# Another order for a hand-ordered attention stage, with the next tile's flags read inside it

## The chip, the cores and the metric

The kernel runs on one core of a Trainium2 chip, as one launch. The core has five engines, each with an instruction queue that is worked off in order: TensorE (PE) multiplies matrices, VectorE (DVE), ScalarE (ACT) and GpSimd (POOL) work on tiles in on-chip memory, and SyncE (SP) issues transfers (DMAs) between the chip's main memory and the tiles; ScalarE and GpSimd can issue transfers too. An engine waits for another by semaphores. The metric is the device time of a launch in microseconds (us), the median of several runs.

## The reference

Three layers follow each other: an attention between x and a small state, in both directions; a mixture of experts, where each row goes to the one expert that its largest logit names; and a dense layer with a gated activation.

```python
# x (4,8,512,64), state (4,8,32,64)
a  = softmax(x @ state.T / 8);  xread = a @ state
a2 = softmax(state @ x.T / 8);  sread = a2 @ x
x = concat([xread, sread], axis=2) -> 2176 rows of 512
# 8 experts, w1 (8,512,1024), w2 (8,1024,512), each takes its first rows up to a capacity
e = argmax(x @ w_gate);  g = softmax(x @ w_gate)[e]
x = g * (relu(x @ w1[e]) @ w2[e])          # rows beyond the capacity are 0
# dense layer, w_in (512,2048), w_out (2048,512)
h = x @ w_in
out = (h * clip(h + 3, 0, 6) / 6) @ w_out
```

## The kernel before

**The stages.** The first, here called the ordered stage, computes the attention for the four batches, writes its rows to the scratch tensor `x_rows`, sorts the rows by expert, and computes the first tile of 256 rows of the mixture. It ends at about 90 us. Then a Python loop over five more tiles of the mixture (`for s in range(N0, NF)`) runs `m1` (L904: rows times w1, in two pieces `q` per group) and `m2` (L922: times w2). Rows that don't fill a tile go in two "pairs", half a tile for each of two experts, with loops of their own (`p_m1` L1254, `p_m2` L1280). The dense layer (L1314, L1352) and the scatter of its rows (L1489) follow from about 240 us on.

**What sets the order.** The ordered stage is written as generators (`tr`, `scores`, `soft_max`, `read_sum`, `lists`, `tables`, `e_m1` and others), each yielding after one or a few instructions. The table `ORDER` names, word by word, which generator takes its next step (`name*3`: three steps); with that an instruction's place in each engine's queue is fixed. Batch b is in the name, as in `tr10` for batch 1. A set of names, `ALT`, chooses the engine of single operations: `mul` and `sub` (L327, L314) and the one-hot tests `oh` (L539) run on VectorE if they are named and else on GpSimd; `rd`, an eviction of attention rows, on VectorE (L404) if named and else on ScalarE (L406); the weight residual `wp` (L827) on GpSimd if named and else on VectorE. Behind the stage the code's own order holds.

**The start.** `inputs` loads the state in two parts with `state_in` (L137): the first quarter `st2[:, 0:2]`, 64 KB, from ScalarE's queue, the rest from SyncE's, between the loads of x (L101, `xb`), which go in pieces of one head. VectorE copies both parts to `aT` (L163, L167); PE transposes the copy (`pst`, L246), VectorE writes it scaled to `sT` (L254), and with `sT` and the transposed x (`psx` L277, copied to `xT` by L279) PE computes the scores (`pss`, L285).

**Weights.** Each tile loads four pieces of w1 (`r0`) and four of w2 (`r1`), 512 KB each, on SyncE (L815, `raw`). ScalarE casts a piece to the reduced format (L825, `w1h` or `w2h`) and a second engine takes the residual (L827, `w1l` or `w2l`), so that a product is three matmuls. Two integers from the table `tab` decide: a flag whether the tile's expert is a new one, and its number. Loads whose flag is zero are skipped, and the split stands in a branch that all engines evaluate. `flags(i)` reads the two integers into SyncE's registers. A pair takes its two experts from the table `tabh` (`p_experts`, L1210) and loads eight pieces of w1, later eight of w2, straight into spare buffers (`p_loads`).

**The end of the stage.** VectorE works the tables out (`tables` up to L709, `halves` up to L782) between the last steps of the first tile, whose result is evicted in two halves (L932) to a tile `y` (here named `xb`) and written by SyncE to the scratch tensor `y_pad` (L938). `next_rows`, `next_turn` and `next_gates` prepare tile 1. Behind the stage, `flags` of tiles 1 and 2, `loads` of `r0`, the first two loads of the dense layer's weights (`vload`, L1112 and L1114, tile `st`), the branch, `r1` of tile 1, `listed`, and `p_begin` with the pair's reads and loads stand in this order.

Of the kernel before, what the change touches and what calls it, by code (L numbers as in the profile page):

```python
# [29 lines left out]
    setup0*4 inputs setup0 tr00 prep_state0 setup2*2 prep_state0*2 setup2*2 setup0 tr00 setup0 tr01 setup2*2 consts tr01 scores00 tr03 tr02 setup2*2  # L30
    inputs zeros setup1 setup3*2 setup1*2 soft_max00 soft_exp00 setup3 setup2 setup1 setup3*2 setup2*2 prep_state2 setup2 turn00 read_max00 setup2
    tr03 e2_turn00 setup2 inputs read_max00 tr02 scores01 e2_turn00 setup2 read_exp00 tr10 turn01 tr11 read_max01 prep_state2 tr10 tr11 setup3
    soft_max01 prep_state2 read_max01 soft_exp01 setup2*2 setup3 setup2 s_read00 read_exp01 prep_state2*2 setup3 setup2 setup3 setup2 inputs s_read00
    read_sum00 s_read00 setup3*2 setup2 read_sum00 read_sum01 prep_state2 scores10 tr12 read_sum00 read_sum01 consts setup2 read_sum01 e2_turn01 tr12
    prep_gate tr20 soft_max10 e2_turn01 tr13 turn10 read_sum00 read_max10 setup3 s_read01 read_sum01 tr20 tr13 prep_gate tr21 soft_exp10 scores11
    inputs s_scale0 tr21 read_max10 s_scale0 read_turn00 read_exp10 read06 setup2 read_turn01 scores20 setup2 turn11 soft_max11 setup3 read_sum10 tr22
    soft_exp11 tr23 read_max11 s_turn0 read_sum10 read_init0 soft_max20 read_max11 read00 turn20 tr22 tr23 read06 read_sum10 read04 scores21 read00
    read07 setup2 s_read10 read_sum10 s_turn0 read05 read_max20 read04 read_exp11 turn21 read01 read07 e2_turn10 read_turn10 read_max21 read_max20
    read03 read05 read02 soft_max21 read_sum11 read_exp20 read01 s_logits0 read_max21 read03 s_read10 setup2 setup3 read02 read10 s_logits0 e2_turn11
    rows_out0 e2_turn10 setup3 read_sum11 read_init1 count0*2 setup3 soft_exp20 count0 e2_turn11 read_sum11 count0 setup3 count0 tr30 s_read10  # L40
    read_sum11 first_expert tr30 before0 first_expert read_exp21 s_logits0 read16 tr31 count0 setup3 first_expert read_sum20 first_expert tr33
    first_expert before0 first_expert s_read11 read_sum20 first_expert read16 tr31 s_scale1 before0 first_expert tr33 first_expert read_turn11 setup3
    total0 soft_exp21 tr32*2 sums0 rows_out0 first_expert read10 place0 scores30 place0 read_sum21 place0 e2_turn20 e2_turn21 s_read20 read12 s_ids0
    place0 read14 read_sum20 s_scale1 place0 soft_max30 turn30 read15 s_scale0 place0 read_sum20 read_init2 read_max30 place0 e2_turn20 read_sum21
    e2_turn21 read_max30 s_turn1 scores31 lists0 read14 read12 s_read20 read15 place0 s_turn1 place0 read_sum21 turn31 soft_max31 lists0 read_max31
    read17 read11 read_sum21 read17 read13 soft_exp30 s_read21 read_exp30 read_turn21 read_turn20 lists0 e2_turn30 early s_logits1 raws lists0 raws
# [554 lines left out]
def full(ctx, tc, x, state, w_gate, w1, w2, capacity, w_in, w_out, out, dbg=None):  # L601
# [343 lines left out]
    def tiles(wk, sm, pS, pT, okp):  # L945
# [703 lines left out]
```

## Time and profile before

| | us |
|---|---|
| median of 3 runs | 559.38 (559.15 to 559.63) |
| the profiled execution | 558.27 |
| its span, first to last instruction | 556.6 |
| PE busy in the span | 525.8 (94%) |
| VectorE busy | 299.5 (54%) |
| ScalarE busy | 217.9 (39%) |
| GpSimd busy | 143.6 (26%) |

The span is what the profiler saw between the first and the last instruction; the execution's own time has 1.7 us round it. The mean granted clock of TensorE is 0.987 of full speed. Shares are averages over three different stages, so what a change in one of them does must be read from that stage: which wait ends last there. "Idle before" in a row is the time that an engine stood still ahead of an instruction, with the name of what let it go.

### The profile page before, as it was taken

The numbers are of one execution on the slowest core, as the hardware profiler recorded it, in microseconds if no ns is written. First come the engines' busy times: TensorE is split into PE (matmuls) and PEld (weight loads), VectorE is DVE, ScalarE is ACT, GpSimd is POOL, SyncE is SP. The second block draws the span as 40 slices with busy tenths as digits, with TensorE's granted clock in tenths as the row PEclk, the third lists the DMA queues.
The fourth block names the chain that finished last, engine by engine and source line by source line (L and its number), as shares of the span: only waits on it lengthen the run. The fifth ranks groups of instructions, "written<-read, shape, count | busy, mean of one in ns | idle before, by whom it ended". The sixth has DMA issues, their size and how long they took to land.

```text
span 556.6 us, 10122 instructions
## 1 busy us (share of the span) xinstructions
PE 525.8 (94%) x3772; PEld 462.8 (83%) x3772; DVE 299.5 (54%) x729; ACT 217.9 (39%) x461; POOL 143.6 (26%) x198
## 2 busy tenths in 40 slices
PE   3899998988999999999999999999999999999990
PEld 1566998958969898999999889999999998888880
DVE  3799894339626763766879852243343343322340
ACT  2788751235214331434443443333333343332340
POOL 1546764113401010136777722001001001000002
PEclk9999999998999999999999999999999999999996
DMA  6727723998989785247653411011001010000001
GB/s 135 179 97 259 253 87 118 315 351 268 378 305 376 253 317 163 77 152 249 228 187 114 134 38 58 1 38 39 1 20 57 1 31 19 21 0 1 0 21 50
DMA packets 52169, 74.99 MB, mean 135 GB/s; under 512 B 23089, under 2 KB 31537, under 8 KB 51602
## 3 DMA queue, kind: packets, MB, share of 16 engines
q1 hardware_dynamic: 49634, 66.83, 36.1%
q0 software_dynamic: 2208, 7.38, 4.0%
q8 instruction: 32, 0.52, 0.4%
q14 instruction: 23, 0.19, 0.1%
q10 hardware_dynamic: 272, 0.07, 0.1%
HBM read 70.62 MB, written 16.23 MB: 156 GB/s over the span
## 4 chain that ended last, share of the span: by engine, by line
issue 35%; PE 26%; DMA 13%; DVE 6%; ACT 2%; POOL 1%; POOLq 0%; SPq 0%; DVEq 0%; ACTq 0%
PE pm L922 8%; PE pm L904 8%; DMA out_dram<-o,fid 5%; PE p L1314 3%; DMA st<-in_moe_w_out_dram 3%; DMA raw<-in_moe_w_dram 3%; PE po L1352 3%; PE pm L1280 2%; DVE v L1128 2%; DVE g L1327 1%; DMA st<-in_moe_w_in_dram 1%; DVE v L1124 1%; DVE v L1126 1%; ACT wh L1142 1%; PE pm L1254 1%
## 5 line engine op out<-in xcount | busy, mean ns | idle before, releaser
L1314 PE MATMUL p<-yT,wh 128*128 128x256 f32 (+1 forms) x768 | 116.7, 294 | 0.0
L1314 PEld LDWEIGHTS p<-yT,wh 128*128 128x128 f32 x768 | 109.1, 188 | 7.8
L1327 DVE SCALAR_TENSOR_TENSOR g<-u,p 128x256 f32<-128x256 f32 x110 | 44.9, 408 | 110.4 <-ACT u L1326 110.2
L1326 ACT ACTIVATE u<-p,b 128x256 f32<-128x256 f32 x110 | 51.2, 466 | 103.6 <-PE p L1314 103.6
L1328 ACT CAST gh<-g 128x256 fp32r<-128x256 f32 x110 | 43.9, 399 | 79.5 <-DVE g L1327 79.5
L1489 POOL DMA_INDIRECT out_dram<-o,fid x14 | 13.9, 996 | 216.1 <-ACT o L1488 190.7
L1314 PE MATMUL p<-yT,wl 128*128 128x256 f32 (+1 forms) x384 | 66.7, 296 | 0.9 <-POOL wl L1143 0.9
L904 PE MATMUL pm<-xt,w1h 128*128 128x256 f32 x320 | 59.1, 286 | 5.0 <-DVE lg L865 2.9
L1352 PE MATMUL po<-wh,gh 128*128 128x512 f32 x156 | 61.2, 392 | 0.0
L1352 PE MATMUL po<-wh,gl 128*128 128x512 f32 x156 | 61.2, 392 | 0.0
L1352 PE MATMUL po<-wl,gh 128*128 128x512 f32 x156 | 61.0, 391 | 0.0
L1314 PEld LDWEIGHTS p<-yT,wl 128*128 128x128 f32 x384 | 55.3, 189 | 2.5 <-POOL wl L1143 1.5
L904 PEld LDWEIGHTS pm<-xt,w1h 128*128 128x128 f32 x320 | 49.9, 192 | 8.4 <-issue 7.8
L1334 DVE TENSOR_TENSOR gl<-g,gh 128x256 fp32r<-128x256 f32 x84 | 34.4, 410 | 32.2 <-ACT gh L1328 32.2
L922 PE MATMUL pm<-hth,w2h 128*128 128x256 f32 x160 | 45.1, 282 | 0.0
L922 PE MATMUL pm<-htl,w2h 128*128 128x256 f32 x160 | 44.8, 280 | 0.0
L922 PE MATMUL pm<-hth,w2l 128*128 128x256 f32 x160 | 44.8, 280 | 0.0
L904 PE MATMUL pm<-xt,w1l 128*128 128x256 f32 x160 | 44.7, 283 | 0.0
L1143 POOL TENSOR_TENSOR wl<-v,wh 128x1024 fp32r<-128x1024 f32 x14 | 34.6, 2471 | 35.7 <-ACT wh L1142 35.4
L1352 PEld LDWEIGHTS po<-wh,gl 128*128 128x128 f32 x156 | 29.3, 188 | 7.1 <-POOL gl L1334 0.6
L1334 POOL TENSOR_TENSOR gl<-g,gh 128x256 fp32r<-128x256 f32 x26 | 24.9, 959 | 30.2 <-ACT gh L1328 30.2
L1352 PEld LDWEIGHTS po<-wl,gh 128*128 128x128 f32 x156 | 29.3, 188 | 3.9
(321 smaller groups left out, 945.4 us busy)
## 6 DMA issues: line engine op xcount, KB each, us to landing
raw<-in_moe_w_dram SPq DMA_DIRECT2D x80, 512.0 KB
st<-in_moe_w_in_dram SPq DMA_DIRECT2D x16, 512.0 KB
st<-in_moe_w_out_dram SPq DMA_DIRECT2D x16, 512.0 KB
x_rows<-xrow SPq DMA_DIRECT2D x4, 1072.0 KB
xb<-in_x_dram SPq DMA_DIRECT2D x32, 128.0 KB
yg<-y_pad SPq DMA_DIRECT2D x13, 258.0 KB
out_dram<-zt SPq DMA_DIRECT2D x2, 1536.0 KB
y_pad<-y SPq DMA_DIRECT2D x5, 516.0 KB
```

What stands on the lines that cost most here:

```text
L904: T.matmul(ps[:, j], W1[l][k][:, ls], xT[r][:, k], start=n == 0, stop=n == 11)
L922: T.matmul(ps[:, j], W2[l][k // 2][:, k % 2, ls], hT[k // 2][r][:, k % 2], start=k == 0 and i == 0, stop=k == 7 and i == 2)
L1128: V.scalar_tensor_tensor(out=t, in0=lo, scalar=29, in1=t, op0=ALU.logical_shift_right, op1=ALU.bitwise_or)
L1143: (V if m in (0, 2) else G).tensor_tensor(out=wl, in0=v, in1=wh.bitcast(F32), op=ALU.subtract)
L1280: T.matmul(ps[s:s + m, :], th[:, a:a + m], raws[k // 2, g][:, 512 * (k % 2) + 256 * n:512 * (k % 2) + 256 * n + w], start=k == 0, stop=k == 7)
L1314: T.matmul(out, w[:, 128 * k:128 * k + 128], r(k), start=n == 0, stop=n == 11)
L1326: A.activation(out=u, in_=ps, func=AF.Relu, bias=b3)
L1327: V.scalar_tensor_tensor(out=g, in0=u, scalar=6.0, in1=ps, op0=ALU.min, op1=ALU.mult)
L1328: A.copy(gh[:, 0:w], g)
L1334: eng.tensor_tensor(out=gl, in0=g[:, 0:n], in1=gh[:, 0:n].bitcast(F32), op=ALU.subtract)
L1352: T.matmul(po[t], l[:, ls], r[:, 512:1024], start=m == 0 and i == 0, stop=m == 15 and i == 2)
L1489: G.indirect_dma_start(out=out, out_offset=bass.IndirectOffsetOnAxis(ap=fid[0:n, t:t + 1], axis=0), in_=o[0:n], in_offset=None, bounds_che ...
```

## The change

The table `ORDER` is written anew, and `ALT` loses thirteen names and gains one: sixteen operations run on another engine. `mul11 mul30 sub30 oh01 oh12 oh20 oh32 oh34` go from VectorE to GpSimd, `oh03` from GpSimd to VectorE, `rd10 rd17 rd31 rd37` from VectorE to ScalarE, and `wp01 wp03 wp11` from GpSimd to VectorE. The reads of the flags of tiles 1 and 2, the (skipped or taken) loads of `r0` of tile 1 and the pair's two expert numbers become steps of the ordered stage (`n_flags`, `n_pair`). The pair's loads are written as a generator but are all drawn in `p_first`, behind the branch, as before. The first tile's `y_pad` write goes from SyncE's to ScalarE's queue, and the buffers of tile 1's rows and of `y` are taken from the pool `xb`, the latter ahead of its matmuls.

```diff
-    setup0*4 inputs setup0 tr00 prep_state0 setup2*2 prep_state0*2 setup2*2 setup0 tr00 setup0 tr01 setup2*2 consts tr01 scores00 tr03 tr02 setup2*2
+    setup2 inputs setup0*3 setup3*2 setup2 setup0*2 inputs setup2*2 tr00 setup2 setup0 tr00 inputs setup0 setup2 prep_state0 setup2 tr01*2
...
 ALT = frozenset("""
-    mul11 mul30 mul31 oh01 oh12 oh20 oh30 oh32 oh34 ol01 ol02 ol10 ol11 ol12 ol21 ol22 ol30 ol33 ol34 rd10 rd17 rd21
-    rd31 rd37 sub30 wp01 wp03 wp11
+    mul31 oh03 oh30 ol01 ol02 ol10 ol11 ol12 ol21 ol22 ol30 ol33 ol34 rd21
 """.split())
...
+        def next_flags():
+            fl[NE] = flags(NE)
+            yield
+            fl[NE + 1] = flags(NE + 1)
+            yield
+            r0[NE] = loads(0, fl[NE])
+
+        def next_pair():
+            pe[pend[0][1]] = p_experts(pend[0][1])
+
         def next_rows():
-            m["n"] = wk.tile([128, 4, 512], F32, name="xT").rearrange("p a b -> p (a b)")[:, 0:2 * ROW].rearrange("p (t c) -> p t c", t=2)
+            m["n"] = big()[:, 0:2 * ROW].rearrange("p (t c) -> p t c", t=2)
...
-            yield from m2_parts(ps, m["h"], q)
             if q == 0:
                 m["y"] = big()[:, 0:2 * YR].rearrange("p (t c) -> p t c", t=2)
+            yield from m2_parts(ps, m["h"], q)
             y_part(m["y"], ps, q, m["gB"])
             if q:
                 yield
-                y_out(m["y"], m["id"], slice(0, 256))
+                V.tensor_copy(m["y"][:, :, DM:YR], m["id"].unsqueeze(2).broadcast_to([128, 2, YR - DM]))
+                yield
+                A.dma_start(out=y_pad[0:256, :].rearrange("(t p) c -> p t c", t=2), in_=m["y"])
...
     def p_first(p):
+        if p in ahead:
+            for _ in ahead.pop(p):
+                pass
+            return
         pe[p] = p_experts(p)
         pr[p] = p_loads(0, pe[p])
...
-    fl = {s: flags(s) for s in (N0, N0 + 1)}
-    r0[N0] = loads(0, fl[N0])
+    ft, pr, pg, pid, pth, py = {}, {}, {}, {}, {}, {}
+    ahead = {}
+    if pend and pend[0][0] == N0 + 1:
+        p = pend[0][1]
+        pr[p] = {}
+        ahead[p] = p_parts(pr[p], 0, pe[p])
+
     vload(0)
```

Line numbers of the changed kernel differ by one or more from those before. The rows that follow are the queues as they are built, an instruction a row, before and after.

ScalarE's queue at the start of the program, before; `aT` is the state, `xT` the transposed x:

```order
L157 ACT_TABLE_LOAD
L157 ACTIVATE onesk<-identk 1x1
L137 DMA aT<-in_state_dram 128x2x64
L279 COPY xT<-psx 128x512 x2
L171 COPY bd<-aT 32x8x64 x2
```

And in the changed kernel:

```order
L136 DMA aT<-in_state_dram 128x2x64
L156 ACT_TABLE_LOAD
L156 ACTIVATE onesk<-identk 1x1
L278 COPY xT<-psx 128x512 x2
L170 COPY bd<-aT 32x8x64 x2
```

The load of the state's first quarter has moved from the third place to the first.

SyncE's queue from the end of the ordered stage to the first branch, before; TENSOR_LOAD is the read of a table entry into a register, ISA belongs to it or to a load's skip:

```order
L413 DMA x_rows<-xrow_179 128x2144
L1367 TENSOR_LOAD tab
L1367 ISA x2
L938 DMA y_pad<-xb 128x2x516
L1368 TENSOR_LOAD tab
L1368 ISA x2
...
L815 DMA raw<-in_moe_w_dram 128x1024
L1112 DMA st<-in_moe_w_in_dram 128x4x256
L1114 DMA st<-in_moe_w_out_dram 128x1024
L1372 TENSOR_LOAD tab
L1372 ISA x2
L1383 COMPARE_AND_BRANCH
```

And in the changed kernel:

```order
L386 DMA x_rows<-xsc_181 64x1x12
L942 TENSOR_LOAD tab
L942 ISA x2
...
L814 DMA raw<-in_moe_w_dram 128x1024
L947 TENSOR_LOAD tabh
L947 ISA x2
L947 TENSOR_LOAD tabh
L947 ISA x2
L1134 DMA st<-in_moe_w_in_dram 128x4x256
L1136 DMA st<-in_moe_w_out_dram 128x1024
L1381 TENSOR_LOAD tab
L1381 ISA x2
L1416 COMPARE_AND_BRANCH
```

The `y_pad` write is gone from this queue, and the two `tabh` reads, which stood behind the branch and the `r1` loads, stand ahead of the `st` loads.

VectorE's queue at the end of the ordered stage, before; `tab` and `tabh` are the tables, L932 evicts the first tile's y, L852 is a correction of tile 1's transposed rows:

```order
L852 TENSOR_TENSOR xt<-psc,xt 128x4x128
L869 TENSOR_TENSOR lg<-lg,gv_115 128x16
L707 TENSOR_SCALAR tab<-ez,es 128x14
L766 SCALAR_TENSOR_TENSOR hr<-Q_81,hr_66 128x8
L768 TENSOR_TENSOR D<-hk,io_72 128x80
L932 TENSOR_TENSOR xb<-pss,gB 128x2x256
L770 TENSOR_TENSOR Z<-D,hr 128x80
...
L879 RECIPROCAL gv_115<-gv_115 128x2
L782 TENSOR_SCALAR tabh<-tabh 128x10
L709 TENSOR_SCALAR tab<-tab 128x14
L1372 TENSOR_LOAD tab
```

And in the changed kernel:

```order
L708 TENSOR_SCALAR tab<-tab 128x14
...
L781 TENSOR_SCALAR tabh<-tabh 128x10
L866 TENSOR_REDUCE gv_115<-lg 128x2
L851 TENSOR_TENSOR xt<-psc,xt 128x4x128
L931 TENSOR_TENSOR xb<-pss,gB 128x2x256
L851 TENSOR_TENSOR xt<-psc,xt 128x4x128
L868 TENSOR_TENSOR lg<-lg,gv_115 128x16
L931 TENSOR_TENSOR xb<-pss,gB 128x2x256
L1042 COPY xb<-idt 128x2x4
```

The last rows of both tables have moved from behind the second eviction of y to places ahead of the first.

## Rows read from the trace of the kernel before

**Rows 1.** The page, part 1: busy us (share of the span) xinstructions.

```profile
PE 525.8 (94%) x3772; PEld 462.8 (83%) x3772; DVE 299.5 (54%) x729; ACT 217.9 (39%) x461; POOL 143.6 (26%) x198
```

**Rows 2.** Waits of TensorE, all of the run: us in total, times, longest.

```profile
PE pst L246 <- DVE aT L163: 4.3, 1, 4.3
...
PE pm L904 <- DVE lg L865: 2.9, 1, 2.9
PE pm L904 <- DVE Z L770: 1.8, 1, 1.8
```

**Rows 3.** Windows, 20 to 80 us: busy (count) by engine, PEclk, DMA share, GB/s.

```profile
20.00:80.00 60.00, 58.29 (x616) 45.94 (x617) 54.71 (x222) 48.69 (x117) 39.14 (x84) 1.00 0.56 183
```

**Rows 4.** Timeline of the start: start, us, what, count [idle before <-releaser].

```profile
3.58 0.62 SPq L137 DMA_DIRECT2D aT<-in_state_dram  x1
...
4.93 1.08 PE L277 MATMUL psx<-identk,xb 128*128 128x128 f32 x4 [4.93 <-DMA xb<-in_x_dram]
...
7.37 0.43 ACTq L137 DMA_DIRECT2D aT<-in_state_dram  x1
...
9.51 17.06 SPq L101 DMA_DIRECT2D xb<-in_x_dram  x24
...
10.05 0.23 DVE L163 COPY aT<-aT 128x128 f32<-128x128 f32 x1 [6.91 <-DMA aT<-in_state_dram]
...
11.05 0.59 DVE L254 TENSOR_SCALAR sT<-pst 64x128 f32<-64x128 f32 x2 [0.78 <-PE pst L246]
...
11.80 1.12 PE L285 MATMUL pss<-xT,sT 128*64 128x512 f32 x1
```

**Rows 5.** Groups by line and shape, VectorE: count | busy, mean ns | idle before.

```profile
L827 DVE TENSOR_TENSOR w1l<-raw,w1h 128x1024 fp32r<-128x1024 f32 x8 | 11.8, 1470 | 17.5 <-ACT w1h L825 17.4
...
L404 DVE COPY xrow<-psX 128x264 f32<-128x264 f32 x5 | 2.1, 421 | 0.1
...
L314 DVE TENSOR_TENSOR R<-R,m 128x512 f32<-128x512 f32 x1 | 0.7, 684 | 0.0
```

**Rows 6.** Timeline of TensorE and SyncE where the ordered stage ends.

```profile
90.06 0.28 PE L922 MATMUL pss<-xb,w2l 128*128 128x256 f32 x1
...
92.26 0.40 SPq L938 DMA_DIRECT2D y_pad<-xb  x1
...
97.66 0.40 SPq L1112 DMA_DIRECT2D st<-in_moe_w_in_dram  x1
...
103.34 0.91 SPq L815 DMA_DIRECT2D raw<-in_moe_w_dram  x2
```

**Rows 7.** Timeline of ScalarE, VectorE and TensorE at tile 2's first half.

```profile
122.37 1.04 ACT L825 CAST w1h<-raw 128x1024 fp32r<-128x1024 f32 x1 [0.24 <-DMA raw<-in_moe_w_dram]
...
125.57 0.68 DVE L932 TENSOR_TENSOR y<-pm,gB 128x512 f32<-128x512 f32 x1
...
126.40 0.55 PE L904 MATMUL pm<-xt,w1h 128*128 128x256 f32 x1 [2.94 <-DVE lg L865]
...
131.31 0.50 PE L904 MATMUL pm<-xt,w1h 128*128 128x256 f32 x2 [0.26 <-DVE y L932]
```

**Rows 8.** Windows in the loop, same columns as rows 3.

```profile
110.00:120.00 10.00, 10.00 (x73) 7.58 (x73) 0.41 (x1) 1.25 (x2) 0.00 (x0) 1.00 1.03 411
...
126.40:129.50 3.10, 3.10 (x14) 3.10 (x15) 2.41 (x15) 1.40 (x4) 0.00 (x0) 0.50 0.84 268
```

**Rows 9.** Chain of waits round tile 4's first half: start, us, what.

```profile
188.07 3.02 PE pm L904 x24
...
191.31 8.48 PE pm L904 x72
```

**Rows 10.** Timeline of SyncE and ScalarE, first tile's second weights.

```profile
55.17 4.03 SPq L815 DMA_DIRECT2D raw<-in_moe_w_dram  x3
...
65.95 4.37 SPq L365 DMA_DIRECT2D x_rows<-sr  x4
...
63.60 1.03 ACT L825 CAST w2h<-raw 128x1024 fp32r<-128x1024 f32 x1
```

More of the change, by code (lines that the diff above doesn't have):

```diff
@@ L62 @@
[L62 to L63 removed]
+    setup2 inputs setup0*3 setup3*2 setup2 setup0*2 inputs setup2*2 tr00 setup2 setup0 tr00 inputs setup0 setup2 prep_state0 setup2 tr01*2
+    prep_state0*2 scores00 tr03 consts tr02 setup1 zeros setup1 soft_max00 setup2 setup1 setup2 prep_state2 tr03 tr02 turn00 prep_state2 setup2
@@ L940, in y_out, with flags, p_experts @@
             nc.sync.dma_start(out=y_pad[row, :], in_=y[:, 0])
+    def flags(i):
+        ch = nc.values_load(tab[0:1, 1, i:i + 1], engines=[ET.SP], min_val=0, max_val=1)
+        e = nc.values_load(tab[0:1, 0, i:i + 1], engines=[ET.SP], min_val=0, max_val=E - 1)
+        return ch, e
+    def p_experts(p):
+        return [nc.values_load(tabh[0:1, 0, 2 * p + g:2 * p + g + 1], engines=[ET.SP], min_val=0, max_val=E - 1) for g in range(2)]
     def lrow(i):
         return nc.values_load(tab[0:1, 2, i:i + 1], engines=[ET.Pool], min_val=0, max_val=NX // 128)
+    fl, pe = {}, {}
+    pend = sorted(PAIRS.items())
     def tiles(wk, sm, pS, pT, okp):
@@ L1206, in m2 @@
         y_out(y, idt, row)
-    def p_experts(p):
-        return [nc.values_load(tabh[0:1, 0, 2 * p + g:2 * p + g + 1], engines=[ET.SP], min_val=0, max_val=E - 1) for g in range(2)]
     def p_rows(p, g):
@@ L1231, in p_xt @@
         return th
-    spare = [(vv, f"v{m}", 1) for m in range(NV - NSP, NV)] + [(vv, "wh0", 1), (vv, "wl0", 1), (mk, "yT0", 2), (mk, "yT1", 2)]
-    def p_loads(which, es_, ks=(0, 2, 1, 3)):
-        bufs = []
-        for pool, tag, n in spare:
-            t = pool.tile([128, 1024 * n], F32, name="raw", tag=tag, bufs=1)
-            bufs += [t[:, 1024 * i:1024 * i + 1024] for i in range(n)]
-        return {(k, g): load(which, es_[g], k, raw=bufs[2 * i + g]) for i, k in enumerate(ks) for g in range(2)}
     def p_first(p):
+        if p in ahead:
+            for _ in ahead.pop(p):
+                pass
+            return
         pe[p] = p_experts(p)
@@ L1364, in accs, with p_parts, p_loads @@
         return [pM.tile([128, 512], F32, name="po", tag="M") for _ in range(2)]
-    def flags(i):
-        ch = nc.values_load(tab[0:1, 1, i:i + 1], engines=[ET.SP], min_val=0, max_val=1)
-        e = nc.values_load(tab[0:1, 0, i:i + 1], engines=[ET.SP], min_val=0, max_val=E - 1)
-        return ch, e
     def new(i):
         return nc.values_load(tab[0:1, 1, i:i + 1], min_val=0, max_val=1)
-    N0 = NE
-    fl = {s: flags(s) for s in (N0, N0 + 1)}
-    r0[N0] = loads(0, fl[N0])
+    spare = [(vv, f"v{m}", 1) for m in range(NV - NSP, NV)] + [(vv, "wh0", 1), (vv, "wl0", 1), (mk, "yT0", 2), (mk, "yT1", 2)]
+    def p_parts(pr, which, es_, ks=(0, 2, 1, 3)):
+        bufs = []
+        for pool, tag, n in spare:
+            t = pool.tile([128, 1024 * n], F32, name="raw", tag=tag, bufs=1)
+            bufs += [t[:, 1024 * i:1024 * i + 1024] for i in range(n)]
+            while len(pr) < len(bufs) // 2 * 2:
+                k = ks[len(pr) // 2]
+                for g in range(2):
+                    pr[k, g] = load(which, es_[g], k, raw=bufs[len(pr)])
+            if len(pr) == 4:
+                yield
+    def p_loads(which, es_, ks=(0, 2, 1, 3)):
+        pr = {}
+        for _ in p_parts(pr, which, es_, ks):
+            pass
+        return pr
+    N0 = NE
+    ft, pr, pg, pid, pth, py = {}, {}, {}, {}, {}, {}
[4 more added lines that the diff above has]
+        ahead[p] = p_parts(pr[p], 0, pe[p])
     vload(0)
@@ L1388, in full @@
     r1[N0] = loads(1, fl[N0])
-    ft, pr, pe, pg, pid, pth, py = {}, {}, {}, {}, {}, {}, {}
-    pend = sorted(PAIRS.items())
     def p_begin():
```

67 lines of the change are left out of this document (33 added, 34 removed).

## The prediction

> **What bounds the kernel now.** I read the page's busy times first, then what TensorE (PE) waited for, then short stretches of the timeline round each of those waits, and last the chain that ended last. PE is busy 525.8 us of a span of 556.6 [rows 1], so about 31 us are all that better timing can return, and what an edit is worth must be read from one of PE's few idle places. Their list is short [rows 2]: 4.3 us for the state tile at the start, 2.9 us before a tile's first matmuls (pm L904 behind the gate work L865), 1.8 us at the end of the ordered stage. The rest of the idle time is the first input load, small waits, and the scatter at the end, which the change doesn't touch. Three terms follow from these three places. A fourth question is the table of order itself: between 20 and 80 us PE is busy 58.29 of 60, VectorE 54.71 and ScalarE 48.69 [rows 3]. There the order can return at most 60 - 58.29 = 1.7 us, and it has more to lose than to win.
>
> **The change part by part. The start.** ScalarE's load of the first quarter of the state leaves at 7.37 [rows 4]. The semaphore that it waits for is the one of SyncE's larger state load, issued at 3.58. VectorE's copy of it starts at 10.05, so 2.7 us after issue, sT follows at 11.05, and the first scores (PE L285) start at 11.80. In the new order the load is ScalarE's first instruction and waits for nothing; by the same 2.7 us it lands at about 3.5, before PE's first x data at 4.93. VectorE's second state copy now stands ahead of sT, so SyncE's load has to be there too: it had landed by 7.37, since that is when the waiting load was let go. The copy is three times as wide as the one of 0.23 us, so 0.3 to 0.7; two sT writes 0.59; from there to the scores 11.80 - 11.64 = 0.16. That gives 7.37 + 0.3 + 0.59 + 0.16 = 8.4 (8.8 at the upper end) in place of 11.80: 3.4 us (3.0). Not all need arrive: the x loads go out at 17.06 / 24 = 0.71 us each until 26.6 [rows 4], a pace that the edit leaves alone, and PE, 3.4 us ahead, may wait for them. I keep 3.0 us, with bounds of 3.4 and, if the x loads or the new order take it all back, 0.
>
> **The order of the stage and the sixteen moved operations.** VectorE loses three 128x512 products or differences at 0.68 us, four evictions at 0.42, five one-hot tests smaller than such an eviction (under 0.42), and gets one such test and three weight residuals at 1.47 [rows 5]: 3 x 0.68 + 4 x 0.42 + 4 x 0.42 = 5.4 removed at the most, 4.4 added, 1 us less in net. ScalarE gets the four evictions, some 1.6 us; GpSimd gets eight of VectorE's operations and loses four, three of them the residuals. None of it can be put on PE's path from the trace, since PE almost never waits here. I price it at nothing: PE is its cover. Bounds: the 1.7 us of PE idle on one side; on the other, a wait for a late operand, which could eat the start's gain (first rival).
>
> **The end of the stage.** PE's last matmul of the stage starts at 90.06 and ends at 90.34; the next starts at 92.15, after 1.81 us [rows 2, 6]. In it VectorE did a transpose correction, a gate step and three table steps before it came to the eviction of y. Now all table steps stand before both evictions of y, and between them stand only one correction and one gate step. An eviction is 0.68 [rows 7], with some 0.5 around it: about 1.3 us remain, a gain of 0.5 (bounds 0 and, if the wait went whole, 1.8).
>
> **The loads behind the stage.** This is the largest term. SyncE is in order. Before, it reached the y_pad write, waited there for y, and issued it at 92.26; only then came the other flag reads, which need VectorE's last table step, four loads of r0 that the flag skips, the first st load at 97.66, the branch, four skipped loads of r1, two tabh reads, and at 103.34 the first load of the pair's first weights [rows 6]. Now y_pad is ScalarE's, and flags, r0 and tabh reads all stand inside the stage, ahead of its end. What is left between stage and pair is st, the branch and r1. St can't go before its buffers come free, which I put at PE's end, 90.34. From st to the pair's first load took 103.34 - 97.66 = 5.7 us, two tabh reads included; that gives 90.34 + 5.7 = 96.0 at the latest, 7.3 us earlier against PE's own place. From there the transfers run at what the DMA engines carry: 411 GB/s from 110 to 120 [rows 8], so an earlier start passes on to all of them; the last of the four first-weight loads of tile 2 stands behind the pair's eight in the same queue. That last load is what holds PE: its cast on ScalarE starts at 122.37, VectorE's residual follows and holds back the y eviction to 125.57, and m1 of tile 2 starts only at 126.40, 2.94 us after PE's previous matmul [rows 2, 7]. After that pause it runs at half pace: the granted clock is 0.50 from 126.4 to 129.5 [rows 8], the lower of the two levels. From 126.40 - 2.94 = 123.46 to its second batch at 131.31 the tile takes 7.85 us [rows 7]; the same piece of tile 4, which waits for nothing, takes 191.31 - 188.07 = 3.24 [rows 9]. The difference is 4.6 us. A lead of 2.9 us is enough to have all casts and residuals done at 123.46, and 7.3 are on offer, so all of it should go, with the low clock, because the pair's 32 matmuls then run into m1 without a pause as in tile 4. What is late next: nothing before the pair's second weights, whose loads queue behind the same ones and move forward with them. Bounds: 0 if the lead is under a microsecond, 4.6 if it is over three. The y_pad write on ScalarE costs one issue of 0.4 us [rows 6] at a place where ScalarE idles; queued behind it is a ReLU that waits for the first 24 matmuls of tile 1, about 3 us [rows 9], so nothing.
>
> **Sum.** 3.0 + 0.5 + 4.6 = 8.1 us. Against the profiled execution of 558.27 that is 550.2; the median of the runs, 559.38, lies 1.1 above it, so 551.3 us.
>
> **A rule that speaks against it.** What the row shows is that the state load leaves late because it waits for a semaphore, not because SyncE was busy [rows 4]. The Trainium skill, page "DMA: Bandwidth & Descriptors", section "Issuing engines are not separate DMA queues", says that loads started from several engines end up on the same 16 DMA engines and interleave, so that spreading their issue only saves issue time. By that rule alone the load on ScalarE would compete with the first x loads and the start's term would be near nothing, the sum 5.1 and the time 554.3, the same as the first rival's; the trace can't show the early load, so it supports this no further.
>
> **The rivals.** (a) *The ordered stage gives the start back.* With VectorE at 91% and ScalarE at 81% [rows 3] a PE that is 3 us early finds operands that are not ready, and a table laid out anew can put a wait where none was. For it: PE can't stay ahead of two engines that are nearly full. Against it: VectorE starts its own work earlier too and has 1 us less of it. The other two terms stay: 559.38 - 5.1 = 554.3. (b) *The pair's loads don't come earlier*: the change doesn't do what it says, since st, or the pair's buffers, still wait for something as late as before (the landing of y_pad, PE's last use of a buffer). For it: the loads still stand behind the branch. Against it: SyncE's time from 92.26 to 97.66 was its own reads and issues, and those are gone. Then 559.38 - 3.5 = 555.9. (c) *Slower: the second weights of the first tile come late.* SyncE's row of writes to x_rows is laid out anew, and the four r1 loads now queue behind three of the four groups of sr writes, where before it was two. Before, they left at 55.17, and ScalarE cast the first at 63.60; the last sr group left from 65.95 to 70.32 [rows 10]. If the sr group ahead of them is ready only when the last one was, they leave at 70.3, 15.1 us later. Of that the cast has at most 63.60 - 55.17 = 8.4 us in hand, less the transfer; with 2.7 us for it (as the state load, [rows 4]) 5.7. The casts stand in front of evictions on ScalarE, so PE would wait 15.1 - 5.7 = 9.4 us: 559.38 - 8.1 + 9.4 = 560.7. It decides the sign once the loads leave more than 5.7 + 8.1 = 13.8 us late, after 69.0. Against it: the sr writes ahead are those of earlier batches. (d) *Both (a) and (b)*, within a microsecond of no change.
>
> **How the numbers follow.** Forecast 0.52, (a) 0.18, (b) 0.10, (c) 0.13, (d) 0.07. The range leaves out (c) and (d). Its lower end takes every term at its best: 3.4 + 1.7 + 1.8 + 4.6 = 11.5, so 547.9. Its upper end is (b) with a start of 2.5 instead of 3.0: 559.38 - 3.0 = 556.4. A difference of about 0.2%, 1.1 us, is what a measurement of this kernel can tell from none. Faster by more are the forecast, (a) and (b): 0.80; same is (d): 0.07; slower is (c): 0.13.
>
> **What would show it.** In the trace of the changed kernel: first scores at 8.4 to 8.8; PE's last matmul of the stage some 3 us before 90.06; a pause of about 1.3 us behind it; the first load of the pair's first weights within 6 us of that; no pause and no granted clock below 1.00 before m1 of tile 2; from the second batch of that tile on, every row some 8 us earlier to the end. The forecast is wrong if the pair's first load keeps its 13 us behind the end of the stage, or if PE's waits between 20 and 90 us grow by more than 2 us.

## The result

The changed kernel takes 550.6 us in the median of its first runs (549.64 to 551.75), the kernel before 559.26 (557.95 to 559.63): a ratio of 0.985, with a 95% interval from 0.9821 to 0.9879. Measured once more on another chip it was 550.48 against 559.67, 0.983 (0.9806 to 0.9855). The forecast was 551.3, so the sum held. Its parts held less well, and the experiments are about them.

The profiled execution took 549.64 us, with a span of 547.9 where it was 556.6. The first line of the page and its busy times, to be set against [rows 1]:

```profile
span 547.9 us, 10114 instructions
...
PE 524.8 (96%) x3772; PEld 461.7 (84%) x3772; DVE 300.1 (55%) x721; ACT 219.0 (40%) x465; POOL 143.0 (26%) x202
```

PE does the same work in less time. All that it waited for, as in [rows 2] (us in total, times, longest):

```profile
PE psx L276 <- DMA xb<-in_x_dram: 5.7, 2, 4.8
PE psc L846 <- DMA xb<-x_rows,ecol: 1.1, 1, 1.1
PE bank L544 <- POOL oh L538: 1.0, 2, 0.8
PE pss L284 <- DVE sT L253: 0.9, 1, 0.9
PE pm L903 <- DVE id L872: 0.9, 1, 0.9
PE p L1328 <- POOL wl L1165: 0.9, 2, 0.7
```

The 4.3 us for the state are gone but for 0.9, the 2.9 us before m1 of tile 2 are gone altogether, and the 1.8 us at the end of the ordered stage are 0.9 (the row that names `id`). Some small ones have come up: 1.1 us for the gathered rows of the first tile, a wait that was not there before, 1.0 us for one-hot tests on GpSimd, where it was 0.5, and 0.9 us for a later load of x (the second of the first row).

**The start** (timeline; start, duration, what), as in [rows 4]:

```profile
0.84 0.42 ACTq L136 DMA_DIRECT2D aT<-in_state_dram  x1
...
3.06 0.16 DVE L162 COPY aT<-aT 128x128 f32<-128x128 f32 x1
...
7.00 0.36 DVE L166 COPY aT<-aT 128x384 f32<-128x384 f32 x1 [2.67 <-DMA aT<-in_state_dram]
...
7.28 0.58 DVE L253 TENSOR_SCALAR sT<-pst 64x128 f32<-64x128 f32 x2
...
8.01 1.97 PE L284 MATMUL pss<-xT,sT 128*64 128x512 f32 x4 [0.88 <-DVE sT L253]
```

ScalarE's load leaves at 0.84, its copy runs at 3.06. VectorE then waits for SyncE's part of the state until 7.00, and the first scores start at 8.01 in place of 11.80, 3.8 us earlier.

**The end of the stage**, as in [rows 6], on TensorE, then SyncE, then ScalarE's queue:

```profile
87.88 0.28 PE L921 MATMUL pss<-xb,w2l 128*128 128x256 f32 x1
89.03 0.35 PE L903 MATMUL pm<-xt,w1h 128*128 128x256 f32 x1 [0.87 <-DVE id L872]
```

```profile
86.96 0.40 SPq L1134 DMA_DIRECT2D st<-in_moe_w_in_dram  x1
87.40 0.52 SPq L1136 DMA_DIRECT2D st<-in_moe_w_out_dram  x1
89.09 15.09 SPq L814 DMA_DIRECT2D raw<-in_moe_w_dram  x16
```

```profile
89.00 0.40 ACTq L1044 DMA_DIRECT2D y_pad<-xb  x1
```

St goes out at 86.96, before PE's last matmul of the stage has started; before it was 7.6 us behind that matmul. Tile 1 starts at 89.03, 3.1 us earlier than 92.15. Of the 3.8 us won at the start the stage has given back 1.6 (PE's last matmul ends at 88.16, before at 90.34: 2.2 earlier); the pause behind it gave 0.9.

**Tile 2**, as in [rows 7] and [rows 9]: ScalarE's last cast, VectorE's two evictions of y, and the chain of waits.

```profile
114.43 1.05 ACT L824 CAST w1h<-raw 128x1024 fp32r<-128x1024 f32 x1 [0.53 <-DMA raw<-in_moe_w_dram]
```

```profile
117.37 0.68 DVE L931 TENSOR_TENSOR y<-pm,gB 128x512 f32<-128x512 f32 x1
...
122.38 0.68 DVE L931 TENSOR_TENSOR y<-pm,gB 128x512 f32<-128x512 f32 x1
```

```profile
113.00 7.02 PE pm L1268 x32
120.02 3.03 PE pm L903 x24
123.05 0.22 PE pgb L889 x2
123.26 8.60 PE pm L903 x72
```

The second batch in the timeline, and the second eviction in the kernel before:

```profile
123.12 0.50 PE L903 MATMUL pm<-xt,w1h 128*128 128x256 f32 x2
```

```profile
130.57 0.68 DVE L932 TENSOR_TENSOR y<-pm,gB 128x512 f32<-128x512 f32 x1
```

The pair's matmuls run into m1 without a pause, and the first batch takes 3.03 us, as in tile 4. From the start of m1 of tile 1 to the second batch of tile 2 the kernel before took 131.31 - 92.15 = 39.2 us; now it is 123.26 - 89.03 = 34.2. So 3.1 us up to tile 1 and 4.9 us up to tile 2 are 8.0 of the span's 8.7; the other 0.7 lies behind that point, most of it in the dense layer (which starts 8.2 us earlier, at 231.06 instead of 239.25) and the scatter, where the code is the same.

One row speaks against the reason given for it, though. The second eviction of y ends at 122.38 + 0.68 = 123.06, and the batch that needs its bank starts at 123.12 (the 123.26 of the chain is the end of the matmuls before it). In the kernel before, where PE waited for this eviction, it ended at 130.57 + 0.68 = 131.25 and the batch started at 131.31, the same 0.06 us later. So there is nothing to spare, where several us were expected.

### The profile page after: what moved, and what is told of

The parts are those of the page before. It is cut to its first block, busy times and chain, and to the rows that moved or that the text cites. A ratio compares the mean times of both kernels' runs of the same rounds, so it can differ in the third digit from the quotient of the medians.

```text
span 547.9 us, 10114 instructions
## 1 busy us (share of the span) xinstructions
PE 524.8 (96%) x3772; PEld 461.7 (84%) x3772; DVE 300.1 (55%) x721; ACT 219.0 (40%) x465; POOL 143.0 (26%) x202
## 4 chain that ended last, share of the span: by engine, by line
PE 44%; issue 36%; DMA 8%; DVE 6%; ACT 2%; SPq 2%; POOL 2%; POOLq 0%; DVEq 0%; ACTq 0%
PE pm L903 11%; PE pm L921 10%; DMA out_dram<-o,fid 5%; PE p L1328 5%; PE po L1366 4%; PE pss L903 2%; PE pm L1294 2%; PE pm L1268 2%; PE pss L921 2%; DVE v L1150 1%; DVE g L1341 1%; SPq L100 1%; PE psX L400 1%; DMA st<-in_moe_w_in_dram 1%; DMA xb<-x_rows,ecol 1%
## 5 line engine op out<-in xcount | busy, mean ns | idle before, releaser
L903 PE MATMUL pm<-xt,w1h 128*128 128x256 f32 x320 | 57.9, 282 | 0.9 <-DVE id L872 0.9
L903 PEld LDWEIGHTS pm<-xt,w1h 128*128 128x128 f32 x320 | 48.8, 188 | 4.0 <-issue 2.9
L1348 DVE TENSOR_TENSOR gl<-g,gh 128x256 fp32r<-128x256 f32 x84 | 34.5, 411 | 32.2 <-ACT gh L1342 32.2
L1165 POOL TENSOR_TENSOR wl<-v,wh 128x1024 fp32r<-128x1024 f32 x14 | 34.4, 2455 | 35.6 <-ACT wh L1164 35.2
L1348 POOL TENSOR_TENSOR gl<-g,gh 128x256 fp32r<-128x256 f32 x26 | 25.4, 975 | 30.2 <-ACT gh L1342 30.2
L1366 PEld LDWEIGHTS po<-wh,gh 128*128 128x128 f32 x156 | 29.4, 188 | 3.8
```

The costliest lines, as they stand in the source:

```text
L903: T.matmul(ps[:, j], W1[l][k][:, ls], xT[r][:, k], start=n == 0, stop=n == 11)
L1165: (V if m in (0, 2) else G).tensor_tensor(out=wl, in0=v, in1=wh.bitcast(F32), op=ALU.subtract)
L1348: eng.tensor_tensor(out=gl, in0=g[:, 0:n], in1=gh[:, 0:n].bitcast(F32), op=ALU.subtract)
L1366: T.matmul(po[t], l[:, ls], r[:, 512:1024], start=m == 0 and i == 0, stop=m == 15 and i == 2)
```

## The experiments

The first theory: three separate terms (the start, the pause at the end of the stage, the loads behind it), the rest nothing. Its rivals: the full stage gives the start back; the gain belongs to other parts of the change than the named ones; what counts behind the stage isn't the loads. In the table every row is one profiled execution. "Scores" is the start of PE's first scores, "tile 1" that of its m1, "cast" how far behind it the last w1 cast of tile 2 starts on ScalarE, "stretch" the time from it to the second batch of tile 2. Medians are of all runs of a kernel; the last column is the median of the kernel before on the same chip.

| kernel | scores | tile 1 | cast | stretch | median | before |
|---|---|---|---|---|---|---|
| before | 11.80 | 92.15 | 30.2 | 39.2 | 559.26 | |
| changed | 8.01 | 89.03 | 25.4 | 34.2 | 550.60 | 559.26 |
| changed, start undone | 12.45 | 92.13 | 25.5 | 34.5 | 553.13 | 558.72 |
| changed, flag reads behind the stage | 8.29 | 89.09 | 24.4 | 34.2 | 549.96 | 558.72 |
| changed, old choice of engines | 7.98 | 95.21 | 25.6 | 34.5 | 556.40 | 558.72 |
| before, state first | 7.37 | 88.21 | 30.4 | 39.4 | 556.66 | 558.72 |
| all code, old order and choice | 7.05 | 89.27 | 31.3 | 40.3 | 555.72 | 560.33 |
| changed, half the pair's loads ahead | 7.85 | 89.39 | 27.0 | 35.6 | 552.50 | 560.33 |
| changed, two more writes of y | 8.03 | 89.92 | 29.5 | 38.8 | 555.44 | 560.33 |
| changed, start and stage trimmed | 7.68 | 88.97 | 26.4 | 35.3 | 549.52 | 560.33 |
| changed, again | 8.04 | 89.76 | 25.3 | 34.2 | 550.48 | 559.67 |
| flag reads behind, again | 7.91 | 89.83 | 24.7 | 34.6 | 550.19 | 559.67 |
| flag reads behind, start trimmed | 7.70 | 88.35 | 25.7 | 34.2 | 549.99 | 559.67 |
| changed, three residuals back | 7.71 | 93.23 | 26.9 | 35.9 | 553.66 | 559.67 |

### The start alone

The changed kernel with the old start:

```diff
-    setup2 inputs setup0*3 setup3*2 setup2 setup0*2 inputs ...
+    setup2 setup0*3 inputs setup3*2 setup2 setup0*2 inputs ...
```

> The changed kernel with ScalarE's state load put back behind the table load and the first activation, where it again waits for a semaphore that SyncE's state load holds; nothing else is moved. Theory (three separate terms): PE's first scores go from 8.01 back to 11.5 or 12, about 1.6 us of that is made up again before the stage ends as it was given back before, so the time is 2 to 3 us above the changed kernel, 552.6 to 553.6. Rival (the stage is bound elsewhere and gives the whole start back): within 0.5 us of the changed kernel, 550.1 to 551.1. In either case the loads behind the stage keep their distance to PE and no pause stands before m1 of tile 2.

Measured: 553.13 us (552.99 to 553.18). The scores start 4.4 us later, tile 1 3.1 us later, and the stretch behind it is the same to 0.3 us. The start is a term of its own, worth 2.5 us against the changed kernel's first runs and 3.2 against the flag reads behind the stage, on the same chip.

The kernel before with the new start:

```diff
-    setup0*4 inputs setup0 tr00 ...
+    inputs setup0*4 setup0 tr00 ...
```

> The kernel before with one edit: the inputs step ahead of setup0, so that ScalarE's state load is its first instruction. Theory (three separate terms): sT on VectorE stands ahead of the second state copy here, so the scores start at 7.5 to 8.5 in place of 11.80; some of the 3.5 us is given back in the stage, 1 to 2 us, so 556.5 to 558 against 559.3. Rival (the old order gives all of it back): 558.8 to 559.8. The pause before m1 of tile 2 stays at about 2.9 us in both.

Measured: 556.66 us, a ratio of 0.9961 to the kernel before (0.9937 to 0.9985), so 2.2 us. In the profiled execution, at 554.41 the fastest of its runs, tile 1 starts 3.9 us earlier and the stretch stays at 39.4; its pause has only been split, 1.5 us for the gate work and 1.6 for the eviction of y. The old order keeps most of what the start gives too. The rival by which the full stage gives it all back is out.

### The flag reads

The changed kernel with the reads where they were:

```diff
-    ... n_flags ... n_flags ... n_flags ... n_pair n_g*2
+    ... n_g*2
...
+    fl.update({s: flags(s) for s in (N0, N0 + 1)})
+    r0[N0] = loads(0, fl[N0])
```

> The changed kernel with the flag reads, the skipped r0 loads and the pair's two expert reads taken out of the ordered stage and written behind it, the expert reads behind r1, as before; y_pad stays with ScalarE and the order of all else stays. Theory 1 (what counts is when VectorE's tables are ready and that SyncE doesn't wait for y; SyncE gets to the reads early wherever the code has them): the pair's loads come at most 1.5 us later against PE, less than the 2.6 us that the y eviction of tile 1 has in hand, so 550.6 to 551.1 as for the changed kernel. Theory 2 (reading the flags inside the stage is what brings the loads forward): the first pair load falls back by 4 us or more, a pause before m1 of tile 2 returns, 553 to 555.5.

Measured: 549.96 us (549.70 to 550.56); on another chip, beside the changed kernel, 550.19 against 550.48. No loss. SyncE reaches code "behind the stage" as soon as its own queue allows, since the wait for y that held it before (`y_pad`) is no longer in that queue. Without the two expert reads ahead of it, st even leaves 1.4 us earlier (85.57), and the cast comes 1 us earlier against tile 1.

All code of the change, the new start too, with the old table of order and the old choice (`e_y1 n_flags*3 n_pair` set behind its last word):

> All code of the change (flags and expert reads as steps of the stage, at its end; y_pad from ScalarE; state load first), but the old table of order and the old choice of engines. Theory 1 (the place of VectorE's last table steps decides when SyncE can read): the reads still wait for L709, VectorE's last step of the stage, about 3.3 us behind PE's end, so the pair's first load stays 10 to 11 us behind the start of m1 of tile 1, the pause before m1 of tile 2 stays, and the time is that of the state load alone, 556.5 to 558. Theory 2 (SyncE's queue, freed of y_pad, brings the loads forward whatever the order): the pause goes, 551.5 to 553.

Measured: 555.72 us against 560.33, 0.9927 (0.99 to 0.9954), so 4.1 us. That is more than the first theory's range and less than the second's; the trace decides. On VectorE, SyncE (its longest wait in the stage, then its timeline) and TensorE:

```profile
90.62 0.17 DVE L709 TENSOR_SCALAR tab<-tab 128x14 int32<-128x14 int32 x1
```

```profile
SPq L944 <- DVE tab L709: 17.4, 1, 17.4
```

```profile
93.27 1.78 SPq L815 DMA_DIRECT2D raw<-in_moe_w_dram  x4
96.61 0.12 SPq L1135 DMA_DIRECT2D st<-in_moe_w_in_dram  x1
```

```profile
124.62 0.36 PE L904 MATMUL pm<-xt,w1h 128*128 128x256 f32 x1 [3.94 <-DVE lg L865]
```

The last table step stands at 90.62, 1.35 us behind the start of tile 1, SyncE's flag read has waited 17.4 us for it, st follows 6.0 us later, and the pause before m1 of tile 2 is 3.94 us, longer than before. So freeing SyncE's queue of `y_pad` isn't enough. What brings the loads forward is the place of VectorE's table steps in the new order, not the place of the reads in the code. No run leaves the `y_pad` write with SyncE in the new order, so what that move is worth by itself isn't measured. The gain is the start's: tile 1 starts 2.9 us earlier, of which the longer stretch takes 1.1 back. The profiled span is 2.6 us shorter than before; where the rest of the 4.1 us of the medians comes from wasn't settled.

### The lead of the loads

The changed kernel, with the first half of the pair's eight loads drawn ahead of st and of the branch:

```diff
         ahead[p] = p_parts(pr[p], 0, pe[p])
+        next(ahead[p])
     vload(0)
```

> The changed kernel with the first four of the pair's eight loads drawn ahead of the two st loads and of the branch. Theory (the lead is saturated: the first tile's y, evicted at 117.37, has 2.6 us in hand before PE wants its bank at 120.02): the casts of tile 2 come 2 to 4 us earlier, PE doesn't, 550.2 to 551.2. Rival (loads ahead of the branch hold up SyncE, so that st comes late and VectorE's conversions of it hold up the residual of the hidden layer behind them): a new pause of PE in m2 of tile 1, 552 to 555.

Measured: 552.50 us, 0.9863 of the kernel before (0.9836 to 0.989); the changed kernel had 0.985 on another chip, so the medians don't separate them. The trace does: the last cast came 1.6 us later against tile 1, not earlier, and the stretch is 1.4 us longer. The time is in the rival's range, but PE doesn't pause in m2 of tile 1, so neither way that was written down is what happened. Waits of SyncE's queue in the changed kernel and in this one (us in total, times, longest), and VectorE's wait in this one:

```profile
SPq L814 <- DMA y_pad<-xb: 4.5, 1, 4.5
```

```profile
SPq L814 <- DMA y_pad<-xb: 7.6, 1, 7.6
```

```profile
101.51 0.43 DVE L1146 TENSOR_SCALAR v<-st 128x512 int32<-128x512 int32 x1 [4.61 <-DMA st<-in_moe_w_in_dram]
```

In both kernels a load of weights waits for the landing of `y_pad`, a write that it has nothing to do with. The built program says why: the transfers of SyncE and ScalarE take eight semaphores in turn, and each is written to wait until the one that had its semaphore before has landed. In the changed kernel the pair's second load has the turn of the `y_pad` write, and leaves at 95.75, 6.75 us after that write was issued; with four loads of 512 KB in flight beside it the write takes longer, SyncE stands for 7.6 us, and the r1 and pair loads behind it leave from 100.35. VectorE also waits 4.6 us for st. This is the answer to "all loads behind the branch": there is nothing to win by half of them ahead.

The changed kernel with 1 MB more of transfers:

```diff
 A.dma_start(out=y_pad[0:256, :]..., in_=m["y"])
+A.dma_start(out=y_pad[256:512, :]..., in_=m["y"])
+A.dma_start(out=y_pad[512:768, :]..., in_=m["y"])
```

> The changed kernel, in which ScalarE writes the first tile's y two more times, to rows that tile 1 and tile 2 write over later: 1 MB more of transfers ahead of the pair's loads, which delays the pair's second load by 3 to 6 us and the last cast of tile 2 by about 2.5 to 5. Theory (the lead over PE has 2.6 us in hand, below that every microsecond is a microsecond of pause, and a pause of some 2 to 3 us costs the low clock as well): with a delay d the time rises by d - 2.6 and 0 to 1.5 us for the clock, 551 to 555. Rival (the pause before was not due to the loads but to VectorE's queue): no rise, 550.2 to 551.2.

Measured: 555.44 us, 0.9909 of the kernel before. The cast is 4.1 us later against tile 1, the stretch 4.6 us longer. The pause is back, and with it the low clock (timeline of TensorE; windows with busy times by engine and, third from the end, the granted clock):

```profile
123.79 0.35 PE L903 MATMUL pm<-xt,w1h 128*128 128x256 f32 x1 [2.48 <-DVE lg L864]
```

```profile
124.00:128.00 4.00, 4.00 (x25) 4.00 (x25) 3.31 (x16) 1.40 (x4) 0.00 (x0) 0.64 0.83 279
```

So the loads are the cause of the pause, and the second reason offered for it is out. The size isn't the theory's: a delay of 4.1 us should have cost 4.1 - 2.6 + 1.5 = 3.0, and it cost 4.6. The 2.6 us were counted from the start of the first eviction of y; from its end, 118.05, to 120.02 there are 2.0. In this run that eviction comes 4.7 us later against tile 1 (33.0 behind it instead of 28.3), and the first batch takes 4.9 us instead of 3.2, 1.7 more. 4.7 - 2.0 + 1.7 = 4.4 is nearly all of the 4.6.

The first eviction isn't the only one that counts. Over the whole table the stretch is 34.2 to 34.6 us while the cast comes within 25.7 us, and 1.1 to 1.7 longer where it comes 26.4 to 27.0 behind. There PE doesn't pause before m1 but before the second batch, here with half the loads ahead:

```profile
125.03 0.50 PE L903 MATMUL pm<-xt,w1h 128*128 128x256 f32 x2 [0.68 <-DVE y L931]
```

What it waits for is the second eviction, which in VectorE's queue comes 5.0 us after the first, behind the gate work and a conversion. By the cast the edge lies between 25.7 and 26.4. By the eviction the changed kernel stood on it in its first profile, and 0.3 us inside it in its second (123.37 and 123.75, where 0.06 is the least). The cast alone doesn't fix it, since what follows it varies. GpSimd and VectorE in the changed kernel, then VectorE with the start undone:

```profile
113.99 2.38 POOL L826 TENSOR_TENSOR w1l<-raw,w1h 128x1024 fp32r<-128x1024 f32 x1 [21.77 <-ACT w1h L824]
```

```profile
115.52 1.93 DVE L826 TENSOR_TENSOR w1l<-raw,w1h 128x1024 fp32r<-128x1024 f32 x1 [1.63 <-ACT w1h L824]
```

```profile
118.71 1.23 DVE L826 TENSOR_TENSOR w1l<-raw,w1h 128x1024 fp32r<-128x1024 f32 x1 [2.42 <-ACT w1h L824]
```

The last residual, just ahead of the first eviction, takes 1.93 us while GpSimd works on another one until 116.37, and 1.23 where it starts at the end of GpSimd's (118.75). The next section is about that.

### The sixteen operations

The changed kernel with the old choice of engines:

> The changed kernel with the old choice of engines for the sixteen operations, in the new order. Theory (the sixteen are covered by PE): within 1 us of the changed kernel, 549.6 to 551.6; the 0.99 us that PE waits near 48 us for one-hot tests on GpSimd go, and as much returns elsewhere. Rival (the new order only works with the new choice): waits of PE between 20 and 90 us grow by more than 2 us, 552.6 or more.

Measured: 556.40 us (0.996 of the kernel before, 0.9934 to 0.9986), 5.8 us more than the changed kernel's first runs and 6.4 more than the flag reads behind the stage on the same chip. The rival's outcome: tile 1 starts at 95.21, the stretch behind it is as short as before. PE's waits in the stage name VectorE, ScalarE and a gather; the longest are 1.6 us (the gather, until 61.09), 1.2 and 1.0 (VectorE). Part of the loss is the clock: the granted clock is 0.59 from 64 to 66 us and 0.78 from 66 to 70, where the changed kernel has 1.00. The trace of VectorE and GpSimd shows what holds VectorE. VectorE, then GpSimd:

```profile
56.33 4.62 DVE L495 TENSOR_TENSOR t<-t,O 128x40 f32<-128x40 f32 x1
```

```profile
56.20 4.66 POOL L827 TENSOR_TENSOR w1l<-raw,w1h 128x1024 fp32r<-128x1024 f32 x2
```

A product of 128x40 elements takes 4.62 us, as long as GpSimd works on two weight residuals beside it, one after the other. In the changed kernel the four instructions of that line take 0.25 us on average. At 76.24 it happens once more: a copy of two columns takes 2.73 us beside the third residual.

The changed kernel with these three residuals alone back on GpSimd:

```diff
-    mul31 oh03 oh30 ... ol34 rd21
+    mul31 oh03 oh30 ... ol34 rd21 wp01 wp03 wp11
```

> The changed kernel with only three of the sixteen operations back: the weight residuals of pieces 1 and 3 of w1 and 1 of w2 on GpSimd. With all sixteen back VectorE's 128x40 product at 56.33 took 4.62 us, the time of two residuals on GpSimd beside it (4.66), and a copy of two columns 2.73 beside the third (2.38). Theory (GpSimd's long two-input operations shut VectorE out while they run): most of the 5.8 us comes back with these three, 554 to 556.5, and in the trace one or two small VectorE operations take over 2 us. Rival (the three are one part of many; evictions and products on VectorE weigh as much): 551 to 553.

Measured: 553.66 us (552.52 to 555.78) beside 550.48, so 3.2 us, between the two expectations. The profiled execution is the longest of its runs; in it tile 1 starts 3.5 us later, and the stretch is 1.7 longer because the cast is late too. VectorE, then GpSimd:

```profile
54.62 4.71 DVE L425 TENSOR_TENSOR sc<-d,W 128x40 f32<-128x40 f32 x1
...
74.90 2.47 DVE L536 TENSOR_SCALAR ol<-io,lo,idmi 128x128 fp32r<-128x128 f32 x1
```

```profile
54.60 4.65 POOL L826 TENSOR_TENSOR w1l<-raw,w1h 128x1024 fp32r<-128x1024 f32 x2
...
74.92 2.36 POOL L826 TENSOR_TENSOR w2l<-raw,w2h 128x1024 fp32r<-128x1024 f32 x1
```

Again one instruction on VectorE, another one than before, lasts as long as the residuals on GpSimd do. So the three residuals are worth 3.2 of the 5.8 to 6.4 us in the median, though their runs scatter by as much; the other thirteen moves would then be worth the 2.6 to 3.2 that are left, by difference, and no run has them alone.

The kernel before had the same three residuals on GpSimd, and VectorE lost nothing by them. One of them, then VectorE beside it:

```profile
59.98 2.37 POOL L827 TENSOR_TENSOR w1l<-raw,w1h 128x1024 fp32r<-128x1024 f32 x1 [0.33 <-ACT w1h L825]
```

```profile
61.02 0.94 DVE L404 COPY xrow<-psX 128x264 f32<-128x264 f32 x2
61.88 0.68 DVE L852 TENSOR_TENSOR xT<-psc,xT 128x512 fp32r<-128x512 f32 x1
```

The copies and the product beside it read matmul results (`psX`, `psc`) and run at their usual length. So it isn't the choice of engine alone that costs, but what the order puts beside it.

The Trainium skill, page "SBUF — State Buffer", section "SBUF: two separate sides", has the rule: VectorE and GpSimd share a pair of ports to the on-chip memory as an exclusive lock, and an instruction of VectorE with two inputs from there is shut out for the whole of an instruction of GpSimd that reads from there too and started first. The trace agrees for the two products, 4.62 beside 4.66 and 4.71 beside 4.65, and there it lasts for two of GpSimd's instructions in a row. The copy (2.73) and the instruction of L536 (2.47) have a single wide input, so this case of two inputs doesn't cover them, and no run shows why they were held.

### Versions that were meant to be faster

Both state loads from ScalarE, one more one-hot test on VectorE, the first tile's transpose two steps later:

```diff
-        load_x(0, 0, 4)
-        state_in(nc.sync, 2, 8)
+        state_in(nc.scalar, 2, 8)
+        load_x(0, 0, 4)
...
-    mul31 oh03 oh30 ...
+    mul31 oh02 oh03 oh30 ...
...
-    count2 e_x0 read35 count2 first_expert place1 read33 s_turn3 e_x0 ...
+    count2 read35 count2 first_expert place1 read33 e_x0 s_turn3 e_x0 ...
```

> A version aimed at what PE still waits for in the changed kernel: both state loads from ScalarE's queue (SyncE's x loads then move up by one place), one more one-hot test of batch 0 on VectorE, and the first step of the transpose of the first tile moved behind two more attention reads. Theory (each wait of PE in the stage is lost time, since PE is busy for the whole of most 20 us stretches): up to 0.5 us of the state wait, 1.0 of the wait for x at 15.06, 1.0 at 48.3 and 1.1 at 57.4 come back, 547.5 to 549. Rival (a full stage gives them back, as it gave back 1.6 of the start's 3.8): 549.8 to 550.8.

Measured: 549.52 us, 0.9798 of the kernel before (0.9769 to 0.9828). In the trace, of the longest of its four runs (550.62), it is the rival: the waits at 48 and 57 us are gone, tile 1 starts at 88.97 as without the edits, and a wait of 1.2 us for VectorE has come up. A late last cast (26.4) put it over the edge besides. Without the one-hot test and with the flag reads behind the stage, for the lead:

> The flag reads behind the stage, both state loads from ScalarE's queue, and the first transpose step of the first tile behind two more attention reads; the one-hot test stays with GpSimd. Theory (the earlier trial of the start's edits lost to a late cast, 26.4 us behind m1 of tile 1, and to a new wait of PE for VectorE that the one-hot test brought): 0.5 to 1.5 us below the changed kernel. Rival (the full stage gives back what the start wins): equal within 0.4 us of the flag reads behind the stage alone.

> The flag reads behind the stage once more. Over the kernels so far the stretch from m1 of tile 1 to the second batch of tile 2 is 34.2 us where the last cast of tile 2 comes at most 25.4 us behind m1 of tile 1, and grows by about a microsecond for each beyond. Here the cast came at 24.4, in the changed kernel at 25.4, just at the edge. Theory (the changed kernel has no lead in hand, and its runs scatter upward where transfers are a little late): this one is 0.3 to 1.0 us faster in the median and scatters less. Rival (the lead of both is enough): equal within 0.3 us.

> The changed kernel once more, beside the three that follow on the same chip. All theories: 549.6 to 551.8, and a second batch of tile 2 that starts 34 to 35 us behind m1 of tile 1.

Measured on one chip: 549.99 us (548.91 to 552.56) for the trimmed start, 550.19 (549.96 to 551.76) for the flag reads alone, 550.48 (549.98 to 551.54) for the changed kernel. The three can't be told apart, as the rivals had it, and the flag reads behind the stage don't scatter less. The best profiled execution is that of the trimmed start (548.91, tile 1 at 88.35), which is a hint and no more. No version was found that beats the changed kernel for certain.

## Why the prediction was right, and where its reasons were not

**The start.** Foretold: scores at 8.4 to 8.8, 3.0 us kept. Measured: 8.01; 2.2 us kept up to the end of the stage, and 2.5 to 3.2 by the run that undoes it. Right, with a size that was a little too large. Of the 1.6 us that the stage gave back, PE's waits behind the first scores account for little: they add up to 3.0 us, before to 2.7. Most of the rest is busy time: from the first scores to its last matmul of the stage PE is busy 76.97 us (8.01 to 88.16), before 75.84 (11.80 to 90.34), with the same matmuls. Why they last longer wasn't settled.

**The order and the sixteen operations.** This step failed. It priced them at nothing, because PE hardly waits in the stage. That is true of either kernel as it is, and says nothing of the pair of them: the new order with the old choice costs some 6 us. What is nothing is the sum of both moves: with the start undone, the new order and the new choice reach tile 1 at 92.13, the old at 92.15, with scores that start 0.65 us later and a last pause that is 0.9 shorter. The step counted VectorE's busy time (4.4 us more, 5.4 less; over the run it rose by 0.6). It didn't ask which of VectorE's instructions would stand beside GpSimd's residuals; a residual costs VectorE 1.2 us in the stage when it does it itself, and some 2.4 when GpSimd does it beside the wrong instruction.

**The end of the stage.** Foretold a pause of 1.3 us instead of 1.8; measured 0.9 in the first profile of the changed kernel and 1.4 in its second. Right.

**The loads.** Foretold 4.6 us, the pause and the low clock; measured 4.9, and the pause and the clock go together, as the run with more writes shows. Three steps of the argument were wrong all the same. It said that 7.3 us of lead were on offer: it was 4.8 (the cast 30.2 us behind tile 1 before, 25.4 now), because the pair's second load waits 4.5 us for the landing of `y_pad`. The pair's first load did leave early, at 90.7, 2.6 us behind PE's end, where 5.7 was foretold. The y write on ScalarE was thus not "nothing"; it was issued early enough to be harmless. It said that 2.9 us of lead were enough: all of the 4.8 was needed, since the second eviction of y follows the first by 5.0 us, behind the gate work, and it looked only at the first. A lead of 7.3 and a need of 2.9 were a margin of 4.4; there was none in the first profile and 0.3 us in the second. And it gave the reads inside the stage a share that belongs to VectorE's table steps. The gain came out right by luck: the lead, smaller than it counted, was just large enough.

**The rivals.** (a) holds for 1.6 of 3.8 us. (b) isn't seen. (c) isn't either: the first tile's r1 loads leave at 52.19, 3.0 us earlier than before, as the whole stage does. The Trainium skill's rule, page "DMA: Bandwidth & Descriptors", section "Issuing engines are not separate DMA queues", that a second queue saves only issue time, was set at 554.3 us. The early load landed within 2.2 us of its issue (0.84 to 3.06), beside the x loads, where the late one took up to 2.7: sharing the engines cost it nothing here, and what was saved was a wait, of which the rule doesn't speak.

## What to carry to other kernels

An order and a choice of engines that were tuned together must be priced together: a stage without waits shows only that they fit. Where a write is issued just ahead of loads, look whose turn of the transfer semaphores they take, and where an eviction frees a bank, follow the queue to the last one that the next matmul needs. Long element-wise work on GpSimd can hold the instruction of VectorE that happens to stand beside it, so put it beside VectorE's reads of matmul results, as the kernel before did, or let VectorE do it. In this kernel one such place is left, the last residual of tile 2, 0.7 us too long just where nothing is to spare; no run moves it.

## What was not expected of the hardware

A write of 516 KB was 6.7 us under way between its issue and the release of the load that waited for it, and with four loads of 512 KB beside it SyncE waited 7.6 us for the same landing. A VectorE product of 128x40 elements took 4.62 us beside GpSimd's residuals, in place of 0.25 on average. And the low clock came without a long pause too: with the three residuals back PE waited only 1.2 and 0.6 us between 56 and 61 us, and the granted clock from 62 to 66 was 0.57 on average, near the lower of the two levels (windows; third from the end). In the changed kernel, with one wait of 1.1 us at 57, it was 1.00 there.

```profile
58.00:62.00 4.00, 3.29 (x28) 2.54 (x27) 3.96 (x18) 3.60 (x8) 2.54 (x11) 1.00 0.52 176
62.00:66.00 4.00, 4.00 (x23) 4.00 (x23) 4.00 (x21) 2.43 (x6) 2.64 (x6) 0.57 0.46 154
```
